# A fused gateloop and feed-forward kernel: one more unit with one-pass products, gate products that no longer wait for the outputs ahead, and earlier loads

## The chip, the cores and the metric

The kernel runs on one core of one Trainium2 chip. The metric is the device time of one execution in microseconds: the median of three runs of the kernel before is 534.78 us (534.14 to 535.33). Beside these runs there is one profiled execution, whose trace is used for everything else. Its engines are TensorE (PE; PEld is its weight load), VectorE (DVE), ScalarE (ACT), GpSimd (POOL) and SyncE (SP), which here only issues DMAs.

## The reference

There are four batches, eight heads, 768 steps and a head width of 48. A linear attention with a complex decay runs over the steps, and its output goes, as 3072 tokens of width 384, through a multiplicative feed-forward block:

```python
mag = sqrt(a_re * a_re + a_im * a_im)
scale = minimum(mag, 0.999) / (mag + 1e-06)
ar, ai = a_re * scale, a_im * scale
for t in range(S):
    S_re, S_im = ar * S_re - ai * S_im + k[t] (x) v[t], ar * S_im + ai * S_re
    y[t] = q[t] . S_re                       # per batch and head, S is 48 x 48
x = y.transpose(0, 2, 1, 3).reshape(3072, 384)
out = ((x @ w1) * (x @ w2)) @ w3 @ w_out     # 384 -> 1024, 1024 -> 1024 -> 384
```

Everything is f32. Since the decay is a product over steps, k can be divided by it and q multiplied by it, with its angle as cosine and sine: within a chunk the step is then ordinary attention with a mask, and between chunks a state is handed on.

## The kernel before, in words

**Units.** The work is cut into eight units, a batch's half each: `TT` = 384 steps in three chunks of `C` = 128. The 384 features stand as three blocks of 128 partitions, in the order feature by head. `w3` and `w_out` are multiplied into one matrix `w3o` at the start (`fuse`). The weights `w1` and `w2` stay on chip as eight tiles `ws`.

**Gates of a unit** (`gates`, `gates_apart`). VectorE and ScalarE work out magnitude, angle and their running sums from `re` and `im` (L645 to L708), multiply k by the inverse decay (L702) and q by the decay (L716), and ScalarE makes cosine and sine. Then come the products with them: k times cosine (L750, into `gR`), q times cosine (L753, into `gA`), k times sine (L758, in place) and q times sine (L764, in place). The cosine is written over `re` and the sine over another tile; `re` and `im` of the next unit are loaded into tiles that these products read (L527, on SP's queue, `load_gates`), so the load of `im` waits for the products with cosine.

**Moves.** By twelve DMAs on SP's queue the four results go, rearranged, into `KL` and `QL`, two tiles of 96 partitions (real and imaginary part) with single buffers, from which TensorE reads; seven DMAs before them put `vr` into `V` (`turn_vr`, L591). k, q and v of the next unit are loaded by GpSimd's queue (`load_of`, `load_v`), and may not start before an instruction of TensorE that is named in the code: in the kernel before, the last output product of the unit ahead, `("y", u - 1)`.

**TensorE's pieces of a unit.** `turn` transposes a chunk's k products (`tp`, L991) and ScalarE copies them to `KT` (L993). `state` multiplies `KT` with `V` (`kv`, L1069) and VectorE adds it to the state `T` (L1075). `scores` (L1004) multiplies `KL` and `QL`, and VectorE copies the result under the mask to `A` (L1007). `outputs` gives y (L1043), which goes out in one of two ways, below. Then come the feed-forward products: `ffn_ab` (x with w1 and w2, `m`, L1089) and `ffn_out` (with `w3o`, L1184), the result of which ScalarE copies to `ot` (L1188) for the store.

**Two forms of x products.** The constant `THREE` says from which unit on they run in the second form. In the first, x is copied by ScalarE (`xT`, L1054) and multiplied in f32 with `ws`; each product takes one evict on ScalarE (L1101) and one multiplication `ab` on VectorE (L1105). In the second, x and the weights are split into two parts of fewer bits: ScalarE writes `x0` (L1047), VectorE the rest (L1050), GpSimd a subtraction (L1051), and the product of the two numbers is the sum of three one-pass products (`wh` is the head of a weight, `low` what is left), with evictions by ScalarE (L1123, L1130) and `ab` again on VectorE (L1105). The weights are split once by `split_ops`: the head by ScalarE (L1152), the rest in two operations on VectorE (L1155, L1157), each 128x768 for one tile. `run` orders the splitting behind the gates of the unit where the second form begins.

**What sets the order.** At build time a planner (`run`) walks through TensorE's pieces in a fixed list (`unit` interleaves the pieces of unit u with the feed-forward products of u-1), keeps estimated clocks for every engine (`TIMES`), and at each piece books gate operations of the next unit (`fill`, `advance`) where their estimated start and end fit before the engine's next duty to TensorE. On each engine, instructions run in the order so written. A generator `gates(u)` yields one operation after another; a yielded "move" makes it stop until unit u-1 has its "end" (`ended[0]`), that is until the pieces of the unit ahead are all written. In the kernel before this word stands ahead of the products with cosine and sine: they, the twelve moves and the loads of the next `re` and `im` between them come only then.

## Time and profile before

| what | value |
| --- | --- |
| median of three runs | 534.78 us (534.14 to 535.33) |
| span of the profiled execution | 534.5 us |
| mean granted clock of TensorE | 0.993 |
| TensorE busy | 498.3 us, 5594 matmuls |
| VectorE busy | 374.7 us |
| ScalarE busy | 325.6 us |
| GpSimd busy | 254.0 us |
| x products begin, units 0 to 7 | 77.78, 138.82, 200.86, 260.38, 317.36, 373.36, 429.77, 486.77 us |
| scores begin, units 2 to 7 | 182.18, 241.58, 295.96, 351.21, 408.51, 464.63 us |
| last move to QL landed, units 2 to 7 | 175.98, 241.34, 294.44, 350.97, 404.85, 459.39 us |
| k issued and landed, units 2 to 7 | 143.77 and 150.03, 199.40 and 204.91, 258.76 and 264.40, 315.27 and 320.80, 369.15 and 375.19, 427.69 and 433.17 us |
| weights split on VectorE | 161.85 to 180.04 us |

All times count from the start of the profiled span. The time up to 77 us is the conversion of the weights, the product `w3o` and the gates of unit 0; then follow the feed-forward products of one unit between the pieces of the next, and from 487 us on the last unit's feed-forward alone. A group of the profile reads: line, engine, operation, tiles with buffer numbers left out, and what ended the idle time before the instruction. In a wait "a <- b" the first is the instruction that waited and the second what it waited for.

### The profile page before, as it was taken

To read this page: it belongs to the slowest core of one execution; us is meant where nothing else is said; L and a number is where in the kernel's file an instruction comes from. 1 tells how busy PE (TensorE), PEld (TensorE's weight loads), DVE (VectorE), ACT (ScalarE), POOL (GpSimd) and SP (SyncE) were. 2 spreads that over 40 slices of the span, in tenths; PEclk is the share of its full clock that TensorE was granted. 3 is DMA by queue.
4 is the path that set the end of the run, shared out by engine and by line. 5 is a ranking of instruction groups with operands and counts; after the bars stand their busy time and mean duration, and the time that the engine had idled before them with its cause. 6 is when DMAs were issued, how large, how long until landed. Compare 5 with 4: busy or idle time off the path is not lost.

```text
span 534.5 us, 13643 instructions
## 1 busy us (share of the span) xinstructions
PE 498.3 (93%) x5594; PEld 378.1 (71%) x5594; DVE 374.7 (70%) x607; ACT 325.6 (61%) x569; POOL 254.0 (48%) x317
## 2 busy tenths in 40 slices
PE   5689889999998999988999999999999998999995
PEld 2355565556655679957888688967896787878972
DVE  7999699855779988756773876577657837336750
ACT  6979866665675458982587557855786554213420
POOL 1000000028968886752664765487457458415510
PEclk9899999999999999998999999999999999999999
DMA  8999859692379219791599239932993176716611
GB/s 258 369 400 286 189 161 307 126 232 72 79 174 229 73 56 234 157 219 40 126 236 216 77 82 245 225 90 70 229 232 87 40 209 169 205 43 189 200 50 37
DMA packets 66424, 89.75 MB, mean 168 GB/s; under 512 B 29872, under 2 KB 53872, under 8 KB 65584
## 3 DMA queue, kind: packets, MB, share of 16 engines
q1 hardware_dynamic: 57904, 59.15, 44.0%
q0 software_dynamic: 8448, 29.63, 20.3%
q8 instruction: 46, 0.75, 0.6%
q14 instruction: 26, 0.21, 0.1%
HBM read 61.01 MB, written 4.72 MB: 123 GB/s over the span
## 4 chain that ended last, share of the span: by engine, by line
PE 51%; DVE 17%; DMA 13%; issue 6%; ACT 5%; POOL 5%; SPq 1%; POOLq 0%; DVEq 0%; ACTq 0%
PE m L1089 24%; PE o L1184 16%; PE y L1043 4%; PE sc L1004 4%; DMA k<-in_k_dram 3%; DMA KL<-k 3%; PE kv L1069 2%; DVE gR L750 2%; PE tp L991 2%; DMA QL<-q 2%; DMA q<-in_q_dram 2%; DMA look<-in_a_re_dram 1%; DVE gA L753 1%; DMA raw<-in_w_dram 1%; POOL look L1327 1%
## 5 line engine op out<-in xcount | busy, mean ns | idle before, releaser
L1184 PE MATMUL o<-w3o,ab 128*128 128x384 f32 x384 | 131.7, 492 | 0.0
L1089 PE MATMUL m<-x,low 128*128 128x384 f32 x576 | 119.2, 339 | 0.0
L1089 PEld LDWEIGHTS m<-x,low 128*128 128x128 f32 x576 | 102.6, 188 | 0.2 <-ACT m L1123 0.2
L1184 PEld LDWEIGHTS o<-w3o,ab 128*128 128x128 f32 x384 | 70.4, 190 | 45.6 <-issue 2.4
L1105 DVE TENSOR_TENSOR ab<-m,ab 128x384 f32<-128x384 f32 x64 | 35.1, 553 | 57.2 <-PE m L1089 39.4
L1089 PE MATMUL m<-x,wh 128*128 128x384 f32 x288 | 69.6, 350 | 3.4 <-ACT ab L1130 2.4
L1123 ACT ACTIVATE m<-m 128x384 f32<-128x384 f32 x96 | 45.5, 476 | 36.0 <-PE m L1089 35.6
L1089 PE MATMUL m<-xT,ws 128*128 128x384 f32 x192 | 63.1, 487 | 1.2 <-ACT xT L1054 1.2
L1328 POOL TENSOR_SCALAR look<-look 128x192 f32<-128x192 f32 (+1 forms) x55 | 54.4, 988 | 5.0
L1089 PEld LDWEIGHTS m<-x,wh 128*128 128x128 f32 x288 | 50.8, 188 | 7.4 <-ACT ab L1130 3.6
L1325 POOL TENSOR_TENSOR look<-look 128x256 f32<-128x256 f32 (+1 forms) x43 | 31.9, 743 | 50.1 <-DMA look<-in_w_dram 32.3
L1089 PEld LDWEIGHTS m<-xT,ws 128*128 128x128 f32 x192 | 36.0, 190 | 25.6 <-ACT xT L1054 1.7
L1273 POOL MEMSET seen<- 128x256 bf16 x1 | 0.3, 317 | 107.7 <-DVE ab L1105 107.7
L1007 DVE COPY_PREDICATED A<-mask,sc 128x512 f32<-128x512 uint8 x48 | 32.8, 734 | 26.5 <-PE sc L1004 26.5
L1289 POOL TENSOR_TENSOR seen<-seen,look 128x192 bf16<-128x192 bf16 (+1 forms) x55 | 44.3, 805 | 4.5
L1051 POOL TENSOR_TENSOR x<-x,x 128x384 fp32r<-128x384 f32 x18 | 23.1, 1284 | 41.7 <-DVE x L1050 41.5
L1188 ACT COPY ot<-o 128x384 f32<-128x384 f32 x24 | 11.4, 476 | 48.4 <-PE o L1184 48.2
L1043 PE MATMUL y<-A,V 128*32 128x128 f32 x768 | 40.2, 276 | 0.6 <-issue 0.6
L1004 PEld LDWEIGHTS sc<-QL,KL 96*32 96x32 f32 x1536 | 29.2, 112 | 13.6 <-issue 8.7
L1004 PE MATMUL sc<-QL,KL 96*32 96x32 f32 (+3 forms) x1536 | 32.8, 238 | 4.4 <-DMA QL<-q 3.0
L1043 PEld LDWEIGHTS y<-A,V 128*32 128x32 f32 x768 | 35.0, 112 | 1.5 <-issue 1.5
L1043 PE MATMUL y<-QL,T 96*32 96x128 f32 x640 | 35.6, 275 | 0.0
(163 smaller groups left out, 909.2 us busy)
## 6 DMA issues: line engine op xcount, KB each, us to landing
looked<-in_w_dram POOLq DMA_DIRECT2D x14, 512.0 KB, 4.5
look<-in_w_dram POOLq DMA_DIRECT2D x27, 256.0 KB, 5.0
raw<-in_w_dram SPq DMA_DIRECT2D x6, 1024.0 KB, 10.3
KL<-gR SPq DMA_DIRECT2D x24, 192.5 KB, 3.6
KL<-k SPq DMA_DIRECT2D x24, 192.5 KB, 7.1
QL<-gA SPq DMA_DIRECT2D x24, 192.0 KB, 8.2
QL<-q SPq DMA_DIRECT2D x24, 192.0 KB, 7.9
raw<-in_w_dram SPq DMA_DIRECT2D x6, 768.0 KB, 6.1
```

Source lines behind the costliest of these rows:

```text
L1004: nc.tensor.matmul(out=sc[SB * g:SB * g + SB, j, s0:C], lhsT=KL[:, x * n + j, w][:, s0:s0 + SB], rhs=QL[:, x * n + j, w][:, s0:C], start=T ...
L1007: last["sc", u, c, x] = nc.vector.copy_predicated(out=A[:, x * n:(x + 1) * n], data=sc, mask=mask)
L1043: nc.tensor.matmul(out=o, lhsT=a, rhs=b, start=s0, stop=s1)
L1051: nc.gpsimd.tensor_tensor(out=x[2], in0=x[1], in1=x[0], op=OP.subtract)
L1089: nc.tensor.matmul(out=out, lhsT=a, rhs=b, start=start and i == 0, stop=i == len(terms) - 1, skip_group_check=not start)
L1105: last["ab", u, j] = nc.vector.tensor_tensor(out=ab_t[u][:, j], in0=m, in1=ab_t[u][:, j], op=OP.mult)
L1123: nc.scalar.activation(out=got[m], in_=got[m], func=AF.Copy, scale=1.0 + 1.0 / BITS)
L1184: nc.tensor.matmul(out=m, lhsT=ab_t[u][:, f, t * P:(t + 1) * P], rhs=w3o[:, f], start=(f == 0), stop=(f == KF - 1))
L1188: nc.scalar.copy(out=o, in_=m)
L1289: nc.gpsimd.tensor_tensor(out=seen[:, 0:n], in0=seen[:, 0:n], in1=x, op=OP.add)
L1325: tt(out=x, in0=x, in1=x, op=OP.mult)
L1328: ts(out=x, in0=x, scalar1=low, scalar2=None, op0=OP.is_ge)
```

## The change

It does four things.

First, `THREE` goes from 2 to 1: unit 1's x products run in the second form too, and the splitting of the eight weight tiles, which stands behind the gates of the unit where that form begins, comes into unit 1's pieces.

Second, the word "move" in the gates is gone, and a word "hold" stands further up, behind the scans. With `HOLDS` = {move: 1, hold: 2} the gates of unit u stop there only until u-2 has ended. The products with cosine and sine are then booked like any gate operation, also before unit u-1's outputs are written.

Third, the moves are collected in one function: V's seven DMAs, then the twelve moves in the order KL<-gR, KL<-k, QL<-gA, QL<-q. It runs at once where unit u-1 has ended, and otherwise at its end. The loads of the next unit's `re` and `im` are no longer between the moves, but where the gates reach them.

Fourth, k, q and v of unit 3 and later are loaded behind the last state product of the unit ahead, `("kv", u - 1)`, by a new piece "loads" in the list of pieces; unit 2's are still behind unit 1's outputs. GpSimd's late loads for its look at the weights wait until the last unit's moves are written.

```diff
@@ -435,7 +435,7 @@
     LOOKS = 2
-    THREE, DEEP = 2, 2
+    THREE, DEEP = 1, 2
     TOP, BITS = 1.0 - 2.0 ** -13, 2.0 ** 12
@@ -569,7 +569,7 @@
         if u > 1:
-            behind(ins, ("y", u - 1))
+            behind(ins, ("kv", u - 1) if u > 2 else ("y", u - 1))
             arrives(("vr", u))
@@ -657,6 +657,7 @@
             act(out=Z[:, s], in_=Z[:, s], func=AF.Copy, scale=-1.0, bias=1.0)
+        yield "hold"
         R = slot(u, "R", "gR")
@@ -728,18 +729,6 @@
         q = g["q"][:, :, 0:TT]
-        yield "move"
-        KL = one.tile([2 * D, H, TT + 1], FP, tag="KL", name="KL")
-        QL = one.tile([2 * D, H, TT], FP, tag="QL", name="QL")
-        L_t[u] = QL, KL, R, g["k"]
-        turn_vr(u)
-        landed("V", (("vr", u),), 2 * LANES - 1, 0.6)
-
-        def move(dst, src, x, i, s, after):
-            for f in range(s.start, s.stop):
-                nc.sync.dma_start(out=dst[x * KD + f::2 * KD], in_=src[:, f])
-            landed("moves", ((after, i),), i + 1, 0.95)
-
         if u < NU - 1:
@@ -748,7 +737,6 @@
             tt(out=r[:, s], in0=k[:, s], in1=re[:, s], op=OP.mult)
-            move(KL, R, 0, i, s, "kc_")
             yield on("DVE", "qc_", i, ("cos_", i), ("q_", i))
@@ -756,14 +744,27 @@
             tt(out=k[:, s], in0=k[:, s], in1=Z[:, s], op=OP.mult)
-            move(KL, g["k"], 1, i, s, "ks_")
-        for i, s in parts:
-            move(QL, A, 0, i, s, "qc_")
         for i, s in parts:
...
             tt(out=q[:, s], in0=q[:, s], in1=Z[:, s], op=OP.mult)
-            move(QL, q, 1, i, s, "qs_")
-        yield None
+        after = [(ready[x, i]) for x in ("kc_", "ks_", "qc_", "qs_") for i in range(2)]
+
+        def moves():
+            KL = one.tile([2 * D, H, TT + 1], FP, tag="KL", name="KL")
+            QL = one.tile([2 * D, H, TT], FP, tag="QL", name="QL")
+            L_t[u] = QL, KL, R, g["k"]
+            clock["SP"] = max(clock["SP"], clock["PE"])
+            turn_vr(u)
+            landed("V", (("vr", u),), 2 * LANES - 1, 0.6)
+            for n, (dst, src, x) in enumerate(((KL, R, 0), (KL, g["k"], 1), (QL, A, 0), (QL, q, 1))):
+                clock["SP"] = max(clock["SP"], *after[2 * n:2 * n + 2])
+                for f in range(KD):
+                    nc.sync.dma_start(out=dst[x * KD + f::2 * KD], in_=src[:, f])
+                landed("moves", (), KD, 0.95)
+        if ended[0] < u - 1:
+            moving.append(moves)
+        else:
+            moves()
 
@@ -978,7 +979,7 @@
             for op in ops:
-                if op is None or op == "move":
+                if op is None or op in HOLDS:
                     break
@@ -1066,7 +1067,7 @@
             for g in range(0, 2 * D, SB):
-                nc.tensor.matmul(out=kv[g:g + SB, hd], lhsT=rows[:, g:g + SB], rhs=V[:, hd], start=True, stop=True)
+                last["kv", u] = nc.tensor.matmul(out=kv[g:g + SB, hd], lhsT=rows[:, g:g + SB], rhs=V[:, hd], start=True, stop=True)
         Tn = Tb[(u * UC + c) % 3]
@@ -1347,6 +1348,8 @@
 
+        while NU - 1 not in L_t:
+            yield 0.5
         for n in range(len(spots) - 1):
@@ -1493,12 +1496,13 @@
 
+        early = [("loads", u + 1)] if 1 < u < NU - 1 else []
         if u % 2:
-            return [[("need", u), tr[0][0]], [tr[0][1]], [kv[0], tr[1][0]], [tr[1][1]], [kv[1]], sc[0], sc[1] + [y[0]],
+            return [[("need", u), tr[0][0]], [tr[0][1]], [kv[0], tr[1][0]], [tr[1][1]], [kv[1]], sc[0] + early, sc[1] + [y[0]],
                     sc[2] + [y[1], y[2], ("end", u)]]
...
             return [[("need", u), tr[0][0]], [tr[0][1]], [kv[0], tr[1][0]], [tr[1][1]], [kv[1], tr[2][0]], [tr[2][1]],
-                    [kv[2]] + sc[0], sc[1] + [y[0]], sc[2] + [y[1], y[2], ("end", u)]]
+                    [kv[2]] + sc[0] + early, sc[1] + [y[0]], sc[2] + [y[1], y[2], ("end", u)]]
         return [[("need", u), tr[0][0]], [tr[0][1]], [tr[1][0], kv[0]], [tr[1][1]], [tr[2][0], kv[1]], [tr[2][1]],
@@ -1540,11 +1544,18 @@
         "db": (("PE", 0.53), ("DVE", 0.56)), "f": (("PE", 1.31),), "f7": (("PE", 1.92), ("ACT", 0.57), ("ACT", 0.57)),
-        "part": (("PE", 2.58),), "half": (("PE", 2.58), ("ACT", 0.48), ("SP", 0.45)), "begin": (), "need": (), "end": (), "judge": ()}
+        "part": (("PE", 2.58),), "half": (("PE", 2.58), ("ACT", 0.48), ("SP", 0.45)), "begin": (), "need": (), "end": (), "judge": (), "loads": ()}
 
...
     held = dict(v=[0.0] * 2, m=[0.0] * 4, sc=[0.0] * 6, tr=[], kv=0, unit=0, h=[])
+
+    HOLDS, moving = dict(move=1, hold=2), []
+
+    def loads(u):
+        load_of(u, "k", ("kv", u - 1) if u > 2 else ("y", u - 1))
+        load_of(u, "q")
+        load_v(u)
 
@@ -1555,10 +1566,10 @@
                 gate["ops"] = gates(gate["u"], False)
-            elif op == "move" and ended[0] < gate["u"] - 1:
+            elif op in HOLDS and ended[0] < gate["u"] - HOLDS[op]:
                 gate["op"] = op
                 return
-            elif op is not None and op != "move":
+            elif op is not None and op not in HOLDS:
                 gate["op"] = op
@@ -1645,7 +1656,7 @@
             while True:
-                op = gate["op"] if gate["op"] != "move" else None
+                op = gate["op"] if gate["op"] not in HOLDS else None
                 for o in urgent:
@@ -1695,12 +1706,15 @@
                     others.extend(s_t["pend"])
-                if 0 < f < NU - 1:
-                    load_of(f + 1, "k", ("y", f))
-                    load_of(f + 1, "q")
-                    load_v(f + 1)
-                if gate["op"] == "move":
+                if f == 1:
+                    loads(2)
+                for o in moving:
+                    o()
+                moving.clear()
+                if gate["op"] in HOLDS:
                     advance()
+            elif kind == "loads":
+                loads(f)
             elif kind == "judge":
@@ -1725,7 +1739,7 @@
             for x in PLAN[k] if k < PLANNED else ():
-                if x == "c" and gate["op"] and gate["op"] != "move":
+                if x == "c" and gate["op"] and gate["op"] not in HOLDS:
                     book(gate["op"])
```

**VectorE, between unit 0's last products and the mask copies of unit 1.** The names `low`, `ws` and `wh` are parts of the weights, `sc` and `A` the scores before and after the mask, `T_122` and `T_123` the state, the others gates of unit 2. Before:

```order
L1075 TENSOR_TENSOR T_122<-kv,T_124 96x8x48
L645 TENSOR_TENSOR im<-im,re 128x768
L647 ISA gZ,st_tan<-im 128x768
L647 ISA st_tan 128x1
L653 SCALAR_TENSOR_TENSOR gA<-gZ,gA 128x384
L653 SCALAR_TENSOR_TENSOR gA<-gZ,gA 128x2x384
L664 TENSOR_SCALAR gA<-gA 128x384
L667 SCALAR_TENSOR_TENSOR gA<-gA,gZ 128x384
L1075 TENSOR_TENSOR T_123<-kv,T_122 96x8x48
L1007 COPY_PREDICATED A_91<-mask,sc_86 128x512
L1007 COPY_PREDICATED A_91<-mask,sc_87 128x512
```

Now (line numbers of the changed kernel: L1106, L1156, L1158, L1076 and L1008 are L1105, L1155, L1157, L1075 and L1007 before), from the last five operations of the splitting on:

```order
L1158 SCALAR_TENSOR_TENSOR low<-wh,low 128x768
L1156 SCALAR_TENSOR_TENSOR low<-ws,wh 128x768
L1158 SCALAR_TENSOR_TENSOR low<-wh,low 128x768
L1156 SCALAR_TENSOR_TENSOR low<-ws,wh 128x768
L1076 TENSOR_TENSOR T_123<-kv,T_122 96x8x48
L1158 SCALAR_TENSOR_TENSOR low<-wh,low 128x768
L1008 COPY_PREDICATED A_91<-mask,sc_86 128x512
L1008 COPY_PREDICATED A_91<-mask,sc_87 128x512
L1008 COPY_PREDICATED A_90<-mask,sc_86 128x512
L1008 COPY_PREDICATED A_90<-mask,sc_87 128x512
L653 SCALAR_TENSOR_TENSOR gA<-gZ,gA 128x384
L653 SCALAR_TENSOR_TENSOR gA<-gZ,gA 128x2x384
```

All sixteen operations of the splitting stand between L1106 and the first mask copy, where before the gate steps L653 to L667 stood, and these come behind the first four mask copies.

**VectorE, at the end of unit 2's gates, during unit 1's x products.** `ab` is the product of the two evicted halves; L708, L702, L716, L750 and L753 are gate steps as told above. Before:

```order
L1105 TENSOR_TENSOR ab<-m,ab 128x384
L691 COPY st_ang<-gZ 128x9
L708 SCALAR_TENSOR_TENSOR gZ<-re,gZ 128x384
L708 SCALAR_TENSOR_TENSOR gZ<-re,gZ 128x768
L1105 TENSOR_TENSOR ab<-m,ab 128x384
L702 TENSOR_TENSOR k<-k,gR 128x384
L702 TENSOR_TENSOR k<-k,gR 128x2x384
L716 TENSOR_TENSOR q<-q,gA 128x384
L716 TENSOR_TENSOR q<-q,gA 128x2x384
```

Now (L709, L703, L717, L739 and L741 are L708, L702, L716, L750 and L753 before):

```order
L1106 TENSOR_TENSOR ab<-m,ab 128x384
L687 SCALAR_TENSOR_TENSOR gZ<-im 128x384
L1106 TENSOR_TENSOR ab<-m,ab 128x384
L687 SCALAR_TENSOR_TENSOR gZ<-im 128x384 x2
L692 COPY st_ang<-gZ 128x9
L709 SCALAR_TENSOR_TENSOR gZ<-re,gZ 128x384
L1106 TENSOR_TENSOR ab<-m,ab 128x384
L709 SCALAR_TENSOR_TENSOR gZ<-re,gZ 128x768
L1106 TENSOR_TENSOR ab<-m,ab 128x384 x2
L703 TENSOR_TENSOR k<-k,gR 128x384
L703 TENSOR_TENSOR k<-k,gR 128x2x384
L717 TENSOR_TENSOR q<-q,gA 128x384
```

Of unit 1's `ab` products, two stood ahead of L702 before (both shown); now six do, the first of them a few rows above these.

**SP's queue, unit 2's moves.** `re` and `im` are the loads for unit 3. Before:

```order
L527 DMA re<-in_a_re_dram 128x3x384
L591 DMA V<-vr 128x6x48
L591 DMA V<-vr 96x6x48
L591 DMA V<-vr 32x6x48
L591 DMA V<-vr 64x6x48 x2
L591 DMA V<-vr 32x6x48
L591 DMA V<-vr 96x6x48
L740 DMA KL<-gR 16x8x385 x3
L527 DMA im<-in_a_im_dram 128x3x384
L740 DMA KL<-k 16x8x385 x3
L740 DMA QL<-gA 16x8x384 x3
L740 DMA QL<-q 16x8x384 x3
```

Now:

```order
L527 DMA re<-in_a_re_dram 128x3x384
L527 DMA im<-in_a_im_dram 128x3x384
L591 DMA V<-vr 128x6x48
L591 DMA V<-vr 96x6x48
L591 DMA V<-vr 32x6x48
L591 DMA V<-vr 64x6x48 x2
L591 DMA V<-vr 32x6x48
L591 DMA V<-vr 96x6x48
L762 DMA KL<-gR 16x8x385 x3
L762 DMA KL<-k 16x8x385 x3
L762 DMA QL<-gA 16x8x384 x3
L762 DMA QL<-q 16x8x384 x3
```

The load of `im` stood behind V's transfers and the first three moves; it now stands ahead of them all.

## The prediction

> **What bounds the kernel now.** I read the page's first lines, then TensorE's own waits in two stretches, then the rows of the places that the change touches.
>
> ```profile
> span 534.5 us, 13643 instructions
> PE 498.3 (93%) x5594; PEld 378.1 (71%) x5594; DVE 374.7 (70%) x607; ACT 325.6 (61%) x569; POOL 254.0 (48%) x317
> ```
>
> TensorE is busy for 93% of the span, and the other engines have slack on average. So the time falls only if TensorE gets less work or waits less. Its waits from 110 to 200 us (unit 1 and the states of unit 2), then those from 200 to 490 us (columns: total, times, longest):
>
> ```profile
> PE kv L1069 <- ACT KT L993: 2.9, 2, 2.2
> PE m L1089 <- ACT xT L1054: 0.6, 1, 0.6
> PE sc L1004 <- DVE A L1007: 0.3, 1, 0.3
> ...
> PE sc L1004 <- DMA QL<-q: 3.0, 1, 3.0
> PE m L1089 <- ACT ab L1130: 2.4, 3, 1.0
> PE tp L991 <- DVE gR L750: 1.6, 3, 0.7
> PE tp L991 <- DVE k L758: 1.0, 2, 0.7
> PE m L1089 <- DVE ab L1105: 0.8, 2, 0.4
> ```
>
> That is 3.8 us in the first stretch and 9.6 us in the second (some rows under 0.5 us are not shown). It is all that better ordering can win; the rest must come from cheaper products.
>
> **The cheaper products.** Unit 1's products with w1 and w2 run as 96 two-part f32 matmuls; the last unit runs the same products as 144 one-pass matmuls. The first row is from the timeline of TensorE, the second from the chain of waits:
>
> ```profile
> 138.82 23.49 PE L1089 MATMUL m<-xT,ws 128*128 128x384 f32 x72 [0.60 <-ACT xT L1054]
> ...
> 487.23 25.46 PE m L1089 x144
> ```
>
> 23.49 / 72 is 0.326 us each, so 96 take 31.3 us; 144 at 25.46 / 144 = 0.177 us take 25.5 us. **Term 1: -5.8 us** (bounds -5 to -6.5: the rate in the other units). [...]
>
> **The splitting, moved into unit 1's pieces.** Before, the eight weights are split on VectorE at 162 to 180 us, during unit 1's products, which ask VectorE only for one `ab` every 3 us. Groups of VectorE's instructions in that stretch:
>
> ```profile
> L1155 DVE SCALAR_TENSOR_TENSOR low<-ws,wh 128x768 fp32r<-128x768 f32 x8 | 8.5, 1057 | 0.0
> L1157 DVE SCALAR_TENSOR_TENSOR low<-wh,low 128x768 fp32r<-128x768 f32 x8 | 8.2, 1031 | 0.2
> ```
>
> The change puts all sixteen ahead of unit 1's first mask copies, where TensorE and VectorE hand work to each other every microsecond. From the timelines of VectorE and TensorE:
>
> ```profile
> 109.24 1.01 DVE L1105 TENSOR_TENSOR ab<-m,ab 128x384 f32<-128x384 f32 x2
> 126.72 1.37 DVE L1007 COPY_PREDICATED A<-mask,sc 128x512 f32<-128x512 uint8 x2 [0.30 <-PE sc L1004]
> ...
> 127.51 1.40 PE L1004 MATMUL sc<-QL,KL 96*32 96x128 f32 x64 [0.31 <-DVE A L1007]
> ```
>
> After 110.25 VectorE has 16.7 us of splits, 3.0 us of L645 and L647 and 1.1 us of L1075 in front of these copies (durations as in that timeline): 20.8 us, so the copies start at 131.05 instead of 126.72, and scores of chunk 1, y and unit 1's products start as much later. **Term 2: +4.2 us.** Lower bound +2.9 (splits at their shortest, 0.95 us); upper +6 (the heads on ScalarE, 0.84 us each, aren't hidden while weights alternate between the engines). It is spread over waits at kv and at scores.
>
> **The gates of unit 2, now behind unit 1's products.** The order shows six `ab` products of unit 1 ahead of L702, where before there were two. The sixth follows 120 one-pass matmuls: 120 x 0.177 = 21.2 us after these products begin. The work behind it, and the transposes that wait for it:
>
> ```profile
> 150.06 1.43 DVE L702 TENSOR_TENSOR k<-k,gR 128x384 f32<-128x384 f32 x2 [2.56 <-DMA k<-in_k_dram]
> 152.70 1.43 DVE L716 TENSOR_TENSOR q<-q,gA 128x384 f32<-128x384 f32 x2 [1.22 <-DMA q<-in_q_dram]
> 154.05 0.55 DVE L750 TENSOR_TENSOR gR<-k,re 128x384 f32<-128x384 f32 x1
> 155.45 1.10 DVE L750 TENSOR_TENSOR gR<-k,re 128x768 f32<-128x768 f32 x1
> 156.47 1.34 DVE L753 TENSOR_TENSOR gA<-q,re 128x768 f32<-128x768 f32 x1
> ...
> 162.15 0.49 PE L991 MATMUL tp<-ident,gR 128*128 128x128 f32 x3
> 169.01 0.88 PE L1069 MATMUL kv<-vr,KT 128*32 128x48 f32 x48 [2.17 <-ACT KT L993]
> ```
>
> 21.2 + 0.56 (`ab`) + 1.43 + 1.43 + 0.55 + 0.55 (L753's first part) + 1.10 = 26.8 us, while TensorE reaches the transposes after 129 matmuls, 22.8 us: a wait of 4.0 us, where before there was none (L750 ended at 156.55, the transposes came at 162.15). Another 1.2 us goes to k (L758) and to the copies KT. The 2.17 us at kv were a wait for copies queued behind the splits and go. **Term 3: +3.0 us** (bounds +2 to +4.2).
>
> **The moves of unit 2.** On SP's queue the load of im, which must wait for the products with cosine (L750, L753), now stands ahead of the seven transfers to V and the twelve moves; before, V and the first moves stood ahead of it. So all of these now begin when L753 ends. What they cost, from SP's queue in unit 2, then unit 3, and the chain of waits of unit 3:
>
> ```profile
> 154.35 4.86 SPq L591 DMA_DIRECT2D V<-vr  x7
> 159.31 1.91 SPq L740 DMA_DIRECT2D KL<-gR  x3
> ...
> 223.54 0.60 SPq L527 DMA_DIRECT2D im<-in_a_im_dram  x1
> ...
> 224.73 8.34 DMA KL<-k
> 233.12 8.22 DMA QL<-q
> ```
>
> In unit 3 the last move landed 17.8 us after im was issued (241.34 - 223.54), with V and gR already out: the lower bound of the new tail. Adding V's and gR's issue in full (4.86 + 1.91) gives 24.6, the upper. I take 19.2: issue of im and V (5.5), some 2.5 to land, and twelve moves at 0.93 (KL<-k at 233.07 to QL<-q at 241.34 is nine in 8.3 us). L753 ends at 26.8 + 1.34 = 28.1 after the products begin, so the last move lands at 47.3. Scores want it at 43.2: before, 20.0 us passed from the first transposes to scores; now 7.8 us of f32 products and the 2.17 go out, 2.7 us of one-pass products, one half of an output (2.6) and 1.2 us of waits come in, from a start at 26.6. A wait of 4.1 us, hidden before behind the V that ran early.
>
> Such a wait costs more than itself. Granted clock (third number from the right) after unit 3's 2.98 us, and the same work at both clocks, from the chain:
>
> ```profile
> 244.00:246.00 2.00, 2.00 (x60) 2.00 (x56) 1.24 (x2) 0.00 (x0) 0.00 (x0) 0.50 0.00 0
> ...
> 243.21 2.20 PE sc L1004 x64
> 250.71 1.25 PE sc L1004 x64
> ...
> 245.42 2.52 PE y L1043 x63
> 469.98 1.76 PE y L1043 x64
> ```
>
> 0.95 + 0.76 = 1.7 us. **Term 4: 4.1 + 1.7 = +5.8 us** (bounds 0 to +11). [...]
>
> **Unit 3.** Its gates no longer wait for the splits, k is there early (loads behind kv of unit 2), and three `ab` stand ahead of L750 instead of five. The third comes 66 x 0.177 = 11.7 us after unit 2's products begin; with 0.56 and some 3.8 us of L750 and L753 that is 16.1, plus 19.2 is 35.3. Scores were wanted at 37.7 (238.60 - 200.86). So the 2.98 us, the clock's 1.7 and a wait of 0.2 go. **Term 5: -4.9 us** (bounds -4.9 to 0).
>
> **Units 4 to 7.** k, q and v arrive some 15 us earlier and im is issued first, so the chain to the cosine is done sooner, and ScalarE's evictions don't queue behind it. In units 5 and 7 one `ab` stands ahead of L750 instead of three: products at 5.3 + 0.56 + 3.7 = 9.5, moves long there. Their waits are 1.1 and 2.3 us (parts of the rows above). In units 4 and 6 three `ab` stand there, and the products stay at 16.1; moves land at 35.3, scores come at 35.6 and 35.1: about even. **Term 6: -3.9 us** (the 3.4 and half a microsecond of unit 6's 1.0; bounds -5.8 to +3).
>
> GpSimd's three subtractions more (about 1.3 us each) stand where it had idle time, and its loads of k for unit 2 still land ten microseconds before L702 comes up; without that cover they would add to term 3.
>
> **Sum**: -5.8 + 4.2 + 3.0 + 5.8 - 4.9 - 3.9 = -1.6 us. The profiled span of 534.5 us is 0.3 under the median of the runs, 534.78; from the median, 533.1 us.
>
> **Rivals.** *A: the tail of moves.* Every microsecond of it over 19.2 is paid three times, in units 2, 4 and 6. At 21.5 us that is +6.9: 540.0; from 20.1 on the change is slower than before. For it: transfers of 7 to 9 us in those rows, and the upper bound. Against it: loads of k, q and v have left that stretch. *B: the splits hide.* If ScalarE and VectorE run them in TensorE's shadow (terms 2 and 3 at their lower bounds) and the tail is 17.8 (term 4 at 2.7 without the clock's share), the sum is -7 : 528. For it: VectorE is busy 16.9 of 28.5 us there; against it: they stand ahead of the copies in order. *C: the one-pass products of unit 1 don't reach their rate,* because each pair now has three evictions on ScalarE instead of one, among unit 2's gates; term 1 is then -3 and the time 536.
>
> **How the numbers follow.** Forecast 0.50 (its own range 531 to 535.5), A 0.27, B 0.13, C 0.10. A measurement here tells a change from none at about 0.2%, 1.1 us: faster means under 533.7, slower over 535.9. Forecast gives 0.31, 0.16, 0.03; A 0, 0.02, 0.25; B 0.13, 0, 0; C 0.01, 0.03, 0.06. Together 0.45 faster, 0.21 the same, 0.34 slower. The range, 529.3 to 538.7, reaches to B and into A.
>
> **What would show it.** Term 1: matmuls m<-x from unit 1 on, 144 in 25.5 us. Term 2: unit 1's mask copies near 131 us, products near 143. Term 3: a wait of tp for L750 of about 4 us near 167. Term 4: a wait of scores for QL<-q near 187, with a granted clock of 0.5 behind it. Term 5: none in unit 3. Term 6: fewer waits after 300 us. Moves landing over 20 us behind im in units 4 and 6 would make the forecast wrong, and so would gates that come earlier than the six `ab` allow.

## The result, and the profile after

The changed kernel takes 579.57 us (median of four runs, 570.80 to 582.86) against 534.46 us before (533.59 to 535.33): a ratio of 1.074, 95% interval 1.067 to 1.081. The ratio is that of the two faster runs (570.80 and 577.70 us) to the runs before, some 40 us; the other two lie over 1.5% above the fastest. The forecast was 533.1, with a range to 538.7. The profiled execution is the slowest of the four, 582.86 us; its span is 581.1 us, 46.6 above the span before, so the readings below add up to more than the 40 us.

The page's first lines, then TensorE's waits over the whole span (columns: total, times, longest):

```profile
span 581.1 us, 13794 instructions
PE 509.4 (88%) x5642; PEld 397.2 (68%) x5642; DVE 378.6 (65%) x607; ACT 332.5 (57%) x585; POOL 253.4 (44%) x324
...
PE sc L1005 <- DMA QL<-q: 12.3, 4, 5.4
PE sc L1454 <- DVE wo_s L1254: 12.0, 4, 6.5
PE sc L1005 <- DMA out_dram<-ot: 8.1, 1, 8.1
PE m L1090 <- DVE ab L1106: 7.4, 6, 1.8
PE tp L992 <- DVE gR L739: 5.7, 4, 3.4
PE y L1044 <- issue: 4.9, 2, 3.5
PE kv L1070 <- ACT KT L994: 4.9, 5, 2.5
PE sc L1005 <- DVE A L1008: 3.4, 3, 2.5
```

Before, scores waited for QL once, 3.0 us; now five times, 20.4 us in all. (The wait of 8.1 us is named after a store, but that store landed only at 209.37, when the scores had run since 207.78. In all five units the scores start 0.24 us after the last move landed.) TensorE is busy 11.1 us longer although unit 1's products are cheaper: the mean granted clock fell from 0.993 to 0.956.

Where the time is, by unit, from the starts of the x products (`m`) in TensorE's timelines:

| from unit | 0 | 1 | 2 | 3 | 4 | 5 | 6 |
| --- | --- | --- | --- | --- | --- | --- | --- |
| before, to the next unit | 61.0 | 62.0 | 59.5 | 57.0 | 56.0 | 56.4 | 57.0 |
| after | 70.2 | 72.5 | 60.7 | 64.8 | 59.0 | 67.1 | 56.0 |
| more | +9.2 | +10.5 | +1.2 | +7.8 | +3.0 | +10.7 | -1.0 |

Another 5.5 us lie ahead of unit 0's x products, where the change moves nothing; they are taken up under the unexpected.

**The tail of moves.** SP's queue in unit 2:

```profile
183.12 0.60 SPq L527 DMA_DIRECT2D im<-in_a_im_dram  x1
183.83 5.53 SPq L591 DMA_DIRECT2D V<-vr  x7
189.45 2.81 SPq L762 DMA_DIRECT2D KL<-gR  x3
192.42 1.87 SPq L762 DMA_DIRECT2D KL<-k  x3
194.39 2.44 SPq L762 DMA_DIRECT2D QL<-gA  x3
197.17 3.27 SPq L762 DMA_DIRECT2D QL<-q  x3
200.97 0.34 SPq L1191 DMA_DIRECT2D out_dram<-ot  x1
```

From im on, which waited for the product q by cosine, twenty transfers (im, seven to V, twelve moves) are issued in 17 us, and the last takes 7.7 us from its issue to land (207.54): 24.4 us from im's issue. In units 3 to 6 the same row takes 24.8, 25.0, 23.8 and 26.8 us. The kernel before had 14.7 to 17.8 there. The chain of waits of unit 3 shows the end of it, and the windows of unit 2 what follows (the third number from the right is the granted clock):

```profile
258.97 9.02 DMA QL<-q
267.99 0.24 issue
268.23 0.82 PE sc L1005 x26
...
190.00:200.00 10.00, 8.94 (x124) 5.61 (x123) 6.02 (x10) 7.65 (x13) 3.96 (x6) 1.00 1.09 218
200.00:208.00 8.00, 0.22 (x5) 0.25 (x9) 0.82 (x2) 2.21 (x3) 0.81 (x1) 0.67 0.97 209
208.00:212.00 4.00, 4.00 (x125) 3.86 (x121) 2.17 (x3) 0.00 (x0) 1.54 (x2) 0.50 0.62 158
```

TensorE stands for eight microseconds, and the next four and more run at half the clock (granted 0.50 from 208 to 212 us).

**The splitting.** ScalarE's timeline in unit 1:

```profile
121.28 0.85 ACT L1153 ACTIVATE wh<-ws 128x768 fp32r<-128x768 f32 x1 [1.03 <-DVE low L1156]
122.03 0.54 ACT L994 COPY KT<-tp 128x384 f32<-128x384 f32 x1
122.45 0.47 ACT L1189 COPY ot<-o 128x384 f32<-128x384 f32 x1
123.15 0.84 ACT L1153 ACTIVATE wh<-ws 128x768 fp32r<-128x768 f32 x1 [0.23 <-DVE low L1156]
123.90 0.54 ACT L994 COPY KT<-tp 128x384 f32<-128x384 f32 x1
```

The copies KT stand behind heads, and each head waits for VectorE, which must have read the tile that the head overwrites. State products of unit 1 wait 2.5 us for these copies and scores 2.5 us for the mask copies; both were under a microsecond before.

### The profile page after: what moved, and what is told of

The parts are those of the page before. It is cut to its first block, busy times and chain, and to the rows that moved or that the text cites. A ratio compares the mean times of both kernels' runs of the same rounds, so it can differ in the third digit from the quotient of the medians.

```text
span 581.1 us, 13794 instructions
## 1 busy us (share of the span) xinstructions
PE 509.4 (88%) x5642; PEld 397.2 (68%) x5642; DVE 378.6 (65%) x607; ACT 332.5 (57%) x585; POOL 253.4 (44%) x324
## 4 chain that ended last, share of the span: by engine, by line
PE 53%; DMA 18%; DVE 13%; ACT 7%; issue 5%; SPq 3%; DVEq 0%; ACTq 0%
PE m L1090 25%; PE o L1185 14%; PE y L1044 7%; DMA QL<-q 6%; PE sc L1005 5%; DMA KL<-k 5%; DMA QL<-gA 3%; DMA V<-vr 2%; DVE gA L741 1%; DVE gR L739 1%; DMA out_dram<-ot 1%; DMA raw<-in_w_out_dram 1%; DVE low L1156 1%; SPq L583 1%; DVE low L1158 1%
## 5 line engine op out<-in xcount | busy, mean ns | idle before, releaser
L1090 PE MATMUL m<-x,low 128*128 128x384 f32 x672 | 142.1, 345 | 0.0
L1185 PE MATMUL o<-w3o,ab 128*128 128x384 f32 x384 | 135.3, 503 | 0.0
L1090 PEld LDWEIGHTS m<-x,low 128*128 128x128 f32 x672 | 122.9, 193 | 0.2
L1185 PEld LDWEIGHTS o<-w3o,ab 128*128 128x128 f32 x384 | 72.5, 196 | 47.5 <-issue 5.9
L1090 PE MATMUL m<-x,wh 128*128 128x384 f32 x336 | 82.9, 356 | 9.0 <-DVE ab L1106 7.4
L1124 ACT ACTIVATE m<-m 128x384 f32<-128x384 f32 x112 | 53.3, 476 | 52.2 <-PE m L1090 50.9
L1106 DVE TENSOR_TENSOR ab<-m,ab 128x384 f32<-128x384 f32 x64 | 35.4, 555 | 72.2 <-PE m L1090 49.7
L1090 PEld LDWEIGHTS m<-x,wh 128*128 128x128 f32 x336 | 60.2, 192 | 14.6 <-DVE ab L1106 10.4
L1008 DVE COPY_PREDICATED A<-mask,sc 128x512 f32<-128x512 uint8 x48 | 33.4, 732 | 49.7 <-PE sc L1005 49.7
L1005 PE MATMUL sc<-QL,KL 96*32 96x64 f32 (+3 forms) x1536 | 36.6, 253 | 24.5 <-DMA QL<-q 12.3
L1005 PEld LDWEIGHTS sc<-QL,KL 96*32 96x32 f32 x1536 | 32.5, 120 | 33.5 <-issue 27.0
L1189 ACT COPY ot<-o 128x384 f32<-128x384 f32 x24 | 11.4, 477 | 63.1 <-PE o L1185 63.1
L1048 ACT ACTIVATE x<-y 128x384 fp32r<-128x384 f32 x21 | 10.3, 490 | 50.7 <-PE y L1044 50.7
L1454 PE MATMUL f<-wo_s,w3s 128*128 128x384 f32 x96 | 34.2, 505 | 0.0
```

Of the source, the lines that this page charges most:

```text
L1005: nc.tensor.matmul(out=sc[SB * g:SB * g + SB, j, s0:C], lhsT=KL[:, x * n + j, w][:, s0:s0 + SB], rhs=QL[:, x * n + j, w][:, s0:C], start=T ...
L1008: last["sc", u, c, x] = nc.vector.copy_predicated(out=A[:, x * n:(x + 1) * n], data=sc, mask=mask)
L1090: nc.tensor.matmul(out=out, lhsT=a, rhs=b, start=start and i == 0, stop=i == len(terms) - 1, skip_group_check=not start)
L1106: last["ab", u, j] = nc.vector.tensor_tensor(out=ab_t[u][:, j], in0=m, in1=ab_t[u][:, j], op=OP.mult)
L1124: nc.scalar.activation(out=got[m], in_=got[m], func=AF.Copy, scale=1.0 + 1.0 / BITS)
L1185: nc.tensor.matmul(out=m, lhsT=ab_t[u][:, f, t * P:(t + 1) * P], rhs=w3o[:, f], start=(f == 0), stop=(f == KF - 1))
```

## The experiments

The theory from these views: the loss is the tail of moves (rival A of the prediction, dearer than it said), and unit 1's splitting beside it. Rivals: D, the loads behind kv take transfer time from the moves; S, the splitting makes all later units late. Ratios below are to the kernel before, measured beside each run on the same chip.

### THREE back at 2

```diff
-    THREE, DEEP = 1, 2
+    THREE, DEEP = 2, 2
```

> The changed kernel with THREE back at 2: unit 1's x products in f32 again, the splitting again in unit 1's products. Moves, hold and loads stay as changed. Theory (the tail of moves: im, V and all twelve moves stand in one row on SP's queue behind the products with cosine, 24 to 25 us from im's issue to the last move): the tails stay at 24 to 25 us and the scores of units 2 to 6 still wait; only unit 1's 9 us and part of unit 2's lateness go: 560 to 568. Rival S (the splitting and the one-pass products of unit 1 make all later units late): under 545. Rival D (the loads of k, q, v behind kv take transfer time from the moves): as the theory, since they stay.

Measured: 577.46 us, ratio 1.076 (1.066 to 1.086), above the 560 to 568 expected. Tails stay at 22.4 to 26.2 us, scores wait up to 11.4 us. S is out: without unit 1's splitting all the loss remains. The ratio didn't fall (1.074 with THREE = 1), though in the trace unit 1 is back at 61.0 us: units 2 to 5 are now 8 to 9 us longer each than before. In unit 2 no score waits; the splitting, which now meets its states, makes kv wait 5.5 us for a copy KT (2.2 before). The scores of units 3 to 5 wait 11.4, 6.9 and 6.4 us for the moves. Why these waits are longer than with THREE = 1 wasn't traced.

### THREE = 1 on the kernel before

> The kernel before with THREE = 1 alone. Theory: moves in the old order, so only unit 1 gets longer, by the nine microseconds seen there less what is made up later: 537 to 545, tails from im to the last move at 14 to 18 us. Rival S: over 560. The sum of the prediction's terms 1 to 3 would give 536.

Measured: 548.77 us, ratio 1.022 (1.013 to 1.030), tails 15.6 to 18.0 us. So this part alone costs about 2%, and more than the theory gave it: 9.4 us in unit 1 (its profile also has a stall ahead of it, as the one after: 2.1 us at 78.58, with a granted clock of 0.50 behind it) and 1 to 1.5 us each in units 2, 4 and 5, while unit 3 is 2.6 us shorter. The prediction's terms 1 to 3 come to +1.4 us; the ratio is 12 us.

### The old order on SP

The edit in outline:

```diff
+        now(first)                      # V, as soon as the unit ahead has ended
         ...  product k by cosine
+            move(0, R, 0, i, s, "kc_")
         ...  product q by cosine, then the load of im, then the other moves
```

> The changed kernel with the old order on SP: V ahead of the products, KL<-gR behind the product k by cosine, then im, KL<-k, QL<-gA, QL<-q. Everything else as changed. Theory: from im's issue to the last move 16 to 18 us instead of 24 to 25, in five units; scores wait 2 us or less; 548 to 556. Rival D: tails stay at 22 or more, 570 or more.

Measured: 549.11 us, ratio 1.022 (1.012 to 1.032), as the theory said. From im's issue to the last move 15.9 to 16.8 us. SP's queue in unit 2, and TensorE's first waits from 170 to 500 us (L759 is the product k by cosine, L1114 is `ab`):

```profile
168.48 5.84 SPq L591 DMA_DIRECT2D V<-vr  x7
179.69 2.67 SPq L752 DMA_DIRECT2D KL<-gR  x3
182.45 0.60 SPq L527 DMA_DIRECT2D im<-in_a_im_dram  x1
183.22 2.25 SPq L752 DMA_DIRECT2D KL<-k  x3
...
PE tp L1000 <- DVE gR L759: 4.9, 3, 3.4
PE m L1098 <- DVE ab L1114: 4.6, 6, 1.8
```

V is out eleven microseconds before the products; no score waits for QL any more. The order of these twenty issues alone is some 28 us of the loss (1.074 against 1.022, on two chips; 1.079 against 1.022 on one, with the next run, whose loads of k, q and v differ too).

### The loads behind y again

One of the four places of the edit:

```diff
-        load_of(u, "k", ("kv", u - 1) if u > 2 else ("y", u - 1))
+        load_of(u, "k", ("y", u - 1))
```

> The changed kernel with k, q and v loaded behind the outputs of the unit ahead again, everything else as changed. Theory: tails 22 to 25 us, since they are set by twenty issues in a row at 0.7 to 0.8 us and by the data of im ahead; time between 572 and 590. Rival D: tails fall to 17 to 19 us and the time to 555 to 562.

Measured: 579.22 us, ratio 1.079 (1.070 to 1.088), tails 22.7 to 25.7 us. As the theory said: the loads don't make the tail.

### What is left: hold and loads

> The changed kernel with both the old order on SP and THREE = 2: what is left of the change is the hold (products with cosine and sine may run before the end of the unit ahead) and the loads of k, q, v behind kv. Theory (the loss is the tail of moves, about 30 us, and unit 1's splitting, about 10): both gone, so the time of the kernel before within 5 us, tails 15 to 18 us. If hold and loads bring what the prediction's terms 5 and 6 say: 5 to 9 us under the kernel before. Rival: hold or loads cost something by themselves: over 5 us above it.

Measured: 541.00 us, ratio 1.010 (1.005 to 1.014). The two largest losses are gone, and what remains brings nothing: it costs 1%, 5 us, at the edge of what was expected. The next two tell which part.

> The changed kernel with THREE = 2, the old order on SP and the loads of k, q and v behind the outputs again: of the change only the hold is left, further up and counted to u-2. Theory now (hold and loads together were 1.0% slower than the kernel before; gates booked further ahead put gate operations in front of the evictions that unit u-1's outputs need): 0.3 to 1.3% slower than before. Rival (the loads behind kv made that 1%): within 0.3%.

Measured: 536.24 us, ratio 1.000 (0.996 to 1.003). The expectation was wrong: the hold alone changes nothing that can be told at 0.4%.

> The kernel before with the loads of k, q and v of units 3 to 7 behind the last state product of the unit ahead, nothing else. Theory: within 0.4% of before, since k had landed before it was asked for there too. Rival D (they take transfer time from the moves to QL, which run at that time): 0.5 to 1.3% slower, with tails 1 to 3 us longer than before. The prediction's terms 5 and 6 in part: up to 1% faster.

Measured: 541.29 us, ratio 1.009 (1.005 to 1.014). The theory was wrong: the loads cost the 1%, though not as rival D has it: the tails are those of before (16.5 to 20.0 us from the product q by cosine, 17.5 to 19.5 before). The longest wait for `ab` stands at 397 us, at unit 6's gates. VectorE there, then TensorE, and below them VectorE at the same place in the kernel before:

```profile
390.65 1.31 DVE L750 TENSOR_TENSOR gR<-k,re 128x768 f32<-128x768 f32 x1
391.88 1.52 DVE L753 TENSOR_TENSOR gA<-q,re 128x768 f32<-128x768 f32 x1
393.33 1.57 DVE L758 TENSOR_TENSOR k<-k,gZ 128x384 f32<-128x384 f32 x2
394.83 1.78 DVE L764 TENSOR_TENSOR q<-q,gZ 128x384 f32<-128x384 f32 x2
396.53 0.54 DVE L1105 TENSOR_TENSOR ab<-m,ab 128x384 f32<-128x384 f32 x1
...
397.13 1.33 PE L1089 MATMUL m<-x,wh 128*128 128x384 f32 x3 [1.73 <-DVE ab L1105]
```

```profile
386.61 1.32 DVE L753 TENSOR_TENSOR gA<-q,re 128x768 f32<-128x768 f32 x1
387.85 0.55 DVE L1105 TENSOR_TENSOR ab<-m,ab 128x384 f32<-128x384 f32 x1
388.32 1.68 DVE L758 TENSOR_TENSOR k<-k,gZ 128x384 f32<-128x384 f32 x2
```

Before, an `ab` stands between the products with cosine and those with sine; with early loads the planner books all four in a row, 6.2 us, and TensorE waits for the `ab` behind them. This wait and the slow products after it (1.33 us for three, as at 431.40 in the changed kernel, where the granted clock was 0.50; there three took 0.79 us at 489.86, at 1.00) are most of the 4.0 us by which the interval from unit 5 to 6 is longer than before. But the next interval is 2.3 us shorter, so this place may explain less than half of the 5 us. The rest is open: it is spread, and in this trace y also stands 2.5 us at 247 for no reason that the profile names. The changed kernel has such waits too (7.4 us at L1106 above).

### What makes the tail: V, or im

With THREE = 2, one edit each: V's transfers ahead of the products, or the load of im behind the moves (V is early then too).

> The changed kernel with THREE = 2 and one edit to the moves: V's seven transfers are issued ahead of the products, as soon as the unit ahead has ended, so that im, then the twelve moves stand behind the products with cosine. Theory: seven issues of 0.7 us go out of the tail, 24.4 becomes 18 to 20 us; the time lies 5 to 15 us above the kernel before (with V behind im it was 38.8 above). Rival (the data of im ahead of the moves make the tail, not the number of issues): tail stays at 22 or more, 30 or more above.

Measured: 561.23 us, ratio 1.044 (1.037 to 1.051). The tail from im's issue is 17.6 to 21.5 us, about as the theory said; the time is not, at some 23 us above the kernel before.

> The changed kernel with THREE = 2 and one other edit: the load of im is issued behind the twelve moves, so that V stands ahead of nothing that waits and goes out early, and no load lies between products and moves. Theory: from the end of the product q by cosine to the last move 14 to 17 us; time within 8 us of the kernel before; the next unit's gates get im some 10 us later. Rival (im's data): the same tail, and 5 us or more better than with V early and im ahead.

Measured: 548.36 us, ratio 1.021 (1.014 to 1.029). From the end of the product to the last move 12.8 to 16.6 us, as the theory said or less; the time, some 11 us above the kernel before, is past the 8 expected.

Since im goes in different places, the tail is taken here from the start of the last product q by cosine to the last move landed. In units 2 to 6 it is 17.5 to 19.5 us before, 25.3 to 28.1 after, 20.4 to 23.0 with V early and 14.2 to 17.6 with im last. The four traces with THREE = 2 and early loads differ only in the edit of SP's order. Their means over units 3 to 6:

| order | tail, us |
| --- | --- |
| im, V, twelve moves ("THREE back at 2") | 25.6 |
| V early, then im, twelve moves | 21.3 |
| V early, KL<-gR, im, nine moves (the old order, in "What is left") | 17.9 |
| V early, twelve moves, im | 15.3 |

So V's seven issues are worth some 4 us of it. The three moves KL<-gR are worth some 3 more where they don't stand behind im: with im last they go out 2.5 to 3.1 us before the product q by cosine ends. And im ahead of the other moves is worth some 3 us, about what three moves of 192 KB take to land (1.02 us apart in unit 2 of the changed kernel), for its 576 KB. In unit 2, where KL<-gR goes out behind the product both with V early and with im last, the two tails differ by 2.9 us. All three make the tail; the rival of either run was in part right. And the shortest tail isn't the fastest kernel, from TensorE's waits with im last (170 to 500 us):

```profile
PE tp L992 <- DVE gR L739: 11.2, 5, 4.6
PE kv L1070 <- ACT KT L994: 2.3, 2, 2.1
```

The load of im is issued 7 to 11 us after the product q by cosine ends, so the next unit's gates get it late, and the transposes wait for the product k by cosine instead.

### Unit 1's splitting, without its parts

Beside THREE = 1:

```diff
-            nc.vector.scalar_tensor_tensor(out=L[:, 0], in0=w, ...)
-            nc.vector.scalar_tensor_tensor(out=L[:, 1], in0=h, ...)
+            nc.gpsimd.memset(L.bitcast(FP), 0.0)
```

> The kernel before with THREE = 1, and the low parts of the weights not worked out: GpSimd sets them to zero, so VectorE's sixteen split operations are gone (the products lose their low part), all else stays. Theory (unit 1 gets longer through the splits ahead of its mask copies): x products of unit 1 start 60 to 62 us after those of unit 0 as in the kernel before, not 70 as with THREE = 1 and the splits, and the run is 5 to 10 us under that with them, about the kernel before. Rival (the one-pass form itself, its three evictions and GpSimd's step cost it): the start stays at 68 or more.

Measured: 534.29 to 544.35 us, median 543.67, too far apart for an interval; only the trace is read. Unit 1's x products start 68.7 us after unit 0's. The theory was wrong, and the rival's sign (68 or more) came true, though the next run shows that the one-pass form is not the reason. In unit 1 the wait for mask copies is gone, that for KT is not:

```profile
PE kv L1069 <- ACT KT L993: 3.2, 1, 3.2
PE m L1089 <- ACT x L1047: 0.9, 1, 0.9
PE sc L1004 <- DVE A L1007: 0.3, 1, 0.3
```

That suggested the heads on ScalarE as the other half:

> The kernel before with THREE = 1, low parts left out (set to zero by GpSimd) and the heads of the weights written by VectorE instead of ScalarE. With the low parts out but the heads on ScalarE the state products still waited 3.2 us for a copy KT. Theory (the heads on ScalarE, in front of the copies KT, are the other half of unit 1's loss): that wait falls to about 1 us, the x products of unit 1 start 61 to 64 us after those of unit 0, those of unit 2 another 56 to 57 us later (one-pass products 5 to 6 us shorter), and the time is 3 to 6 us under the kernel before. Rival (the one-pass form of unit 1's outputs costs it): the start stays at 66 or more.

```profile
PE m L1089 <- ACT x L1047: 1.0, 1, 1.0
PE sc L1004 <- DVE A L1007: 0.8, 1, 0.8
PE kv L1069 <- ACT KT L993: 0.7, 1, 0.7
```

Measured: 62.0 us from unit 0 to unit 1 (61.0 before), 57.7 from 1 to 2 (62.0 before): the heads are the other half (the trace before this one also has a stall of 3.2 us at unit 0 and a mean granted clock of 0.976, against 0.990 here; I put that at about a microsecond of its 68.7). The 4.3 us from 1 to 2 are near what the cheaper products were to bring. Yet the time is 537.00 us, ratio 0.999 (0.994 to 1.004), not the 3 to 6 us under it that I expected. They are lost again, for the most part in unit 4's gates, from TensorE and VectorE there:

```profile
264.21 1.19 PE L1089 MATMUL m<-x,wh 128*128 128x384 f32 x3 [2.68 <-ACT ab L1130]
...
261.27 1.43 DVE L702 TENSOR_TENSOR k<-k,gR 128x384 f32<-128x384 f32 x2 [7.57 <-DMA k<-in_k_dram]
```

VectorE stands 7.6 us at the product with k, whose load is behind unit 3's outputs and lands at 261.25; a step of ScalarE needs what VectorE does next, and the evict L1130 stands behind that step. The interval from unit 3 to 4 is 61.4 us instead of 57.0.

### Half a step, in unit 3 alone

The edit in outline:

```diff
-            load im of the next unit (ahead of KL<-k)
+            load im of the next unit (behind KL<-k, in unit 3 alone)
```

> The kernel before with one row moved: in unit 3 alone the load of im stands behind the three moves KL<-k. The scores of unit 3 waited 2.98 us for the last move there and lost 1.7 us to the clock. Theory (data of im ahead of the moves lengthen the tail): tail from the product q by cosine 17 to 18 us instead of 19.3, the wait falls to 1 us or less, and 2 to 4 us come off; unit 4's gates get im 2 us later, which costs up to 1. Rival (transfers stay as late, since im's data only change places with KL<-k): no change.

Measured: 536.59 us, ratio 1.001 (0.997 to 1.005). In the profile the 2.98 us wait is down to 1.3 us, and the tail is 17.7 us; its span is 531.1, its mean granted clock 0.992 (0.993 before). So the tail moved as the theory said, but the 2 to 4 us are not in the runs: the interval leaves room for a gain of 1.6 us at most.

## Why the prediction was wrong

The losses, taken off one after another (ratio to the kernel before): changed kernel 1.074; with the old order of moves 1.022; with THREE = 2 as well 1.010; with the loads behind y as well 1.000. What the hold is worth lies within 0.4%.

| term | predicted | measured |
| --- | --- | --- |
| 1, one-pass products of unit 1 | -5.8 | 120 products in 21.8 us, 0.181 each: -5.2 |
| 2, splits ahead of the mask copies | +4.2 (2.9 to 6) | +7.0 with an undisturbed unit 0 (68.0 against 61.0, loads behind y) |
| 3, gates of unit 2 behind six `ab` | +3.0 | tp waits 3.4 + 1.3 = 4.7 us (predicted 4.0), less 2.2: +2.5; with the slow clock behind them (granted 0.54 and 0.60 from 182 to 186 us) +6.6 (THREE = 1 alone, where no score waits for a move: unit 2 is 1.4 longer, of which term 1 is -5.2) |
| 4, moves of unit 2 | +5.8 | +9.1, unit 2's +10.5 less that 1.4 (wait 8.1 us, 4.1 predicted) |
| 5, unit 3 | -4.9 | +1.2 |
| 6, units 4 to 7 | -3.9 | +20.5 |

**The step that failed is the tail of moves, 19.2 us**, in the words of the prediction "issue of im and V (5.5), some 2.5 to land, and twelve moves at 0.93". It measured 24.4 in unit 2. Of the 5.2 us more, the issue of im and V is 0.7 (6.2 us) and the moves 1.1 (landings 1.02 us apart). Here I had counted wrong: from 233.07 to 241.34 nine moves land, but between them lie eight steps, 1.03 us each. The other 3.4 are the 2.5, which was 5.9: im takes 5.9 us from issue to landing, V's transfers land behind it, the last at 195.28, 5.9 us after the end of their issue, and the moves behind those. I had taken a landing as a constant at the end of a row of issues, where it is a second row with its own rate. The bound of 24.6 held in unit 2 and was passed in units 3, 4 and 6 (24.8, 25.0, 26.8). I put the value near its lower end, after the row of unit 3, in which V and gR had gone out early. The profile before had that warning: im took 6.3 to 8.9 us to land in units 2 to 6, and three of the four groups of moves 7.1 to 8.2 us. The products themselves came nearly when predicted: q by cosine ended 29.5 us after the x products began for unit 2 (28.1 predicted) and 17.1 for unit 3 (16.1).

**Terms 5 and 6 rest on the same number.** With 24 to 25 us the waits that were to go came back larger. They come in each unit from 2 to 6, not in three of them: 8.1, 2.2, 3.4, 1.3 and 5.4 us, the longer ones in even units, where the prediction had the moves come late. Rival A was thus what happened; its time was too low (540.0 at 21.5 us; by its own rule three times 5.2 us more would be 549), since it counted three units and left out the slow clock, the heads on ScalarE and the cost of the early loads.

**What early loads were to bring** (term 6: "the chain to the cosine is done sooner, and ScalarE's evictions don't queue behind it") they didn't: by themselves they cost 1%. In unit 6 that is because the planner packs the products closer and an `ab` falls behind them; for the rest the cause is open.

**Term 2** had the mechanism on VectorE right and left the half on ScalarE in its upper bound: heads that wait for VectorE, ahead of the copies KT. Its size of 6 there was still 1 us short; that the half clock after one of the two waits of 2.5 us (the one that ends at 133.90, with 0.50 granted from 134.90 on) makes the difference is argued, not shown. (Two slips of a tenth in the working change nothing: 131.05 less 126.72 is 4.3, and 534.78 less 1.6 is 533.2.)

**Right** were term 1, the wait of term 3 (not the slow clock behind it, which it left out), the place of each wait (tp for L750, scores for QL<-q), and the condition named as what would make the forecast wrong: moves landing over 20 us behind im.

## What to carry to other kernels

On SP's queue here an issue that waited held up all that stood behind it (in unit 2 V's issues began at 183.83 us behind im, and at 168.48 with the old order), so what needs nothing (V) should stand ahead of it; twenty transfers behind one late product were 28 us, and seven transfers moved ahead are worth some 4 us of the tail in each unit (25.6 to 21.3 us). To price a row of transfers like this one, add up two rows, issues and landings, and take the later (in unit 2 the issues were out by 200.44, and the last landing came at 207.54); a load of 576 KB ahead of moves of 192 KB counted like three of them here (2.9 us in unit 2). When parts of a change hide behind each other, take them off one after another: THREE back at 2 brought nothing with the long tail, and 6 us without it (1.022 to 1.010).

## What was not expected of the hardware

**The clock after short waits.** In nine of these traces (the two of the comparison, THREE back at 2, THREE = 1 alone, the old order, loads behind y, hold alone, V early, im last), from 60 us on, all 22 waits of TensorE of 2.98 us and more were followed by a granted clock of 0.50, within two microseconds and for three or more. Of 34 waits from 1.27 to 2.65 us, 16 were (the shortest of them have further gaps beside them; waits inside a slow stretch that an earlier one began are not counted). Waits of the same length go either way: a wait of 2.51 us for a copy KT in unit 1 has the slow clock behind it in the changed kernel (at 124.50) and not with the loads behind y (at 118.36). In the changed kernel one of 2.51 us that ends at 140.64 has it, and one of 2.21 us that ends at 268.23 has not:

```profile
138.00:140.00 2.00, 0.13 (x11) 0.00 (x0) 2.00 (x4) 0.93 (x2) 1.92 (x2) 1.00 0.16 49
142.00:144.00 2.00, 2.00 (x23) 1.22 (x12) 1.62 (x4) 0.15 (x1) 1.78 (x3) 0.50 0.15 49
...
266.00:268.00 2.00, 0.01 (x1) 0.00 (x0) 0.69 (x1) 0.52 (x1) 0.00 (x0) 1.00 0.99 226
270.00:272.00 2.00, 2.00 (x100) 1.98 (x99) 1.72 (x4) 0.00 (x0) 0.10 (x1) 1.00 0.92 223
```

What decides it was not shown. The length alone doesn't: a wait of 1.85 us that ends at 307.84 in the changed kernel has a granted clock of 0.50 behind it, and one of 2.65 us that ends at 446.82 with THREE back at 2 has 1.00. In the profile after, the slow clock is about a third of the loss, by an estimate: 11.1 us more of busy time and 5.2 us of cheaper products make 16 of 46.6. It may also be why runs of one kernel with such waits lie 10 us apart: of the four runs after, the shortest has a mean granted clock of 0.969 and the two longest 0.956. That it is the cause is argued, not shown.

**A stall of TensorE ahead of unit 0's x products.** In the profile after, y stands 3.5 us there ("issue": nothing in the profile names a cause), and the clock is halved for 6 us (granted 0.50 from 80 to 86 us): most of the 5.5 us ahead of unit 0. The change leaves the program as it was at that place. The same place shows 0.6 us before, 3.2 with the low parts left out, 1.45 with the loads behind y and 0.6 with the hold alone. It differs from trace to trace where the program is the same, so it isn't a part of the change; its cause stays open.
